# Loading and transposing x by row tile at the start of a cached-attention kernel

## The chip, the core and the metric

The kernel runs on one core of a Trainium2 chip. The metric is the device time of one execution in microseconds. A profile is one further execution with the hardware profiler on; its times are in microseconds from the start of its span.

## What is computed

The reference is attention over the last W keys of a cache, with a projection in front and one behind. All tensors are bf16.

```python
B, Sq, D = 8, 32, 1024;  Hq, Hkv, Sk, Dh = 32, 4, 8192, 128
W = min(4096, max(256, Sk // 4))                     # 2048
q = (x @ wq).reshape(B, Sq, Hq, Dh).transpose(0, 2, 1, 3)
k = repeat(k_cache[:, :, Sk - W:, :], Hq // Hkv, axis=1)   # v alike
p = softmax(einsum("bhqd,bhkd->bhqk", q, k) * Dh ** -0.5)
o = einsum("bhqk,bhkd->bhqd", p, v)
return o.transpose(0, 2, 1, 3).reshape(B, Sq, Hq * Dh) @ wo
```

x has 256 rows (8 batches of 32) of 1024 values, so it is two row tiles of 128 rows.

## The kernel before

The work is cut into 32 units, one for each pair of KV group g and batch b, with all batches of a group in a row. A unit has 16 key tiles of 128, taken in four chunks of four. A chunk is four score matmuls (L467), one exponential on ScalarE (L469), and eight matmuls that apply the result to the values (L478). The value matmuls of a chunk are queued two chunks behind its scores. Beside them the loop in `run` puts in other TensorE work at fixed places: transposes of K for the next unit (`k_pieces`, L236), the q projection of later groups (`q_pieces`, L275) and the output projection (`o_pieces`, L295).

The order of every engine's instructions is the order in which the program writes them (`manual_schedule`). Nearly all loads are issued on SP's queue, one behind the other; `start` writes down the first ones: x, the eight c-blocks of `wq` for group 0 in seven pieces (L164: four of one block, one of two, two of one), K and V of the first units (L188, L193, L204). One half of x goes over ScalarE's queue instead. An issue on SP can wait until an earlier transfer has landed or until a buffer is free, and everything behind it on SP then waits too. K of units 0 to 4 is loaded as it is and transposed on TensorE; K of unit 4 is read by the pieces at L236 during unit 3.

`start` is the part around the change. Ahead of any data, TensorE runs eight matmuls on constants (`warm_up`, L346) into a PSUM tile `warm_ps`. x is in `x_sb`, 128 rows of each row tile on the partitions. `x_turn` (L350) transposes it in blocks of 128 × 128: a c-block takes the columns c, c + 8, c + 16 and so on. The first call does c = 0 to 3 of both row tiles into one PSUM tile, the second c = 4 to 7 into another; in each, VectorE copies the first two c-blocks to `xT` and ScalarE the other two (L357). Then come the q matmuls of group 0 (L375): for c = 0 to 7, eight heads each, with `wq` as the stationary and `xT` of both row tiles as the moving operand, and into four PSUM tiles of two heads (L361). For c = 6 and 7 (`Q_CUT`) only row tile 0 is done at first, and the rest of it in `q_rest`. Ahead of c = 6 the first half of unit 0's K is transposed (`k_turn`, L368).

PSUM comes from three pools of two buffers, `ps_m` (tag `m`), `ps_o` and `ps_s` (tag `s_ps`). A buffer is handed out again when all readers of its last tile are done. `warm_ps` has one of `ps_s`; the first `xT_ps` has one of `ps_m`, the second the other of `ps_s`.

Of the kernel before, what the change touches and what calls it, by code (L numbers as in the profile page):

```python
# [11 lines left out]
BF16 = mybir.dt.bfloat16  # L12
# [4 lines left out]
RL_LIMIT = 1.0e22  # L17
RL_MIN = 1.0e-10
Q_CUT = 6
N_WARM = (8, 0, 0)  # L20
VA_ROW = 160
V_HALVES = 30

# [81 lines left out]
class Fast:  # L105
# [206 lines left out]
    def start(self):  # L312
        nc, P = self.nc, self.P
        warm = self.ps_s.tile([P, 512], FP32, name="warm_ps", tag="s_ps")
        one = nc.const_aps.tensor
        x_sb = self.vp.tile([P, self.NT, self.D], BF16, name="x_sb", tag="v")
        xf = self.x.rearrange("b s d -> (b s) d")
        H = self.DC // 2

        nc.sync.dma_start(out=x_sb[:, 0, :], in_=xf[0:P, :])  # L320
        nc.scalar.dma_start(out=x_sb[:, 1, :], in_=xf[P:2 * P, :])
        wq0 = self.load_wq(0, 0, (1, 1, 1, 1)) + self.load_wq(0, 1, (2, 1, 1))
        for p in wq0[:5]:
            p()
        self.load_k(0, 0)
        wq0[5]()
        wq0[6]()
        self.load_k(0, 1)
        self.load_v(0, nc.sync)
        self.load_k(1)  # L330
        self.load_v(1, nc.sync)
        self.weights = []
        for g in range(self.Hkv):
            if g + 1 < self.Hkv:
                self.weights += self.load_wq(g + 1, 0) + self.load_wq(g + 1, 1)
            if g:
                self.weights += self.load_wo(2 * g - 2) + self.load_wo(2 * g - 1)
        self.weights += self.load_wo(2 * self.Hkv - 2) + self.load_wo(2 * self.Hkv - 1)
        for ui in range(2, 4):
            self.load_unit(ui)  # L340
        for v in self.va:
            nc.gpsimd.memset(v[:, :, self.Dh:self.VW], 1.0)
        nc.gpsimd.memset(self.ones_c[:, :], 1.0)
        def warm_up(n):
            for i in range(n):
                nc.tensor.matmul(warm[:, :], lhsT=one(1.0, [P, P], BF16), rhs=one(1.0, [P, 512], BF16), start=True, stop=True)  # L346
        warm_up(N_WARM[0])


        def x_turn(half, pl, tag):  # L350
            ps = pl.tile([P, H, self.NT, P], BF16, name="xT_ps", tag=tag)
            for c in range(H):
                for t in range(self.NT):
                    nc.tensor.transpose(ps[:, c, t, :], x_sb[:, t, half * H + c:self.D:self.DC], self.ident[:, :])
            for i, copy in ((0, nc.vector.tensor_copy), (1, nc.scalar.copy)):
                c0 = half * H + i * H // 2
                copy(out=self.xT[:, c0:c0 + H // 2, :], in_=ps[:, i * H // 2:(i + 1) * H // 2, :, :].rearrange("p c t s -> p c (t s)"))  # L357

        x_turn(0, self.ps_m, "m")
        x_turn(1, self.ps_s, "s_ps")  # L360
        qs = [pl.tile([P, 2, self.NQ], FP32, name="q0_ps", tag=tag)  # L361
              for pl, tag in ((self.ps_o, "o_ps"), (self.ps_o, "o_ps"), (self.ps_m, "m"), (self.ps_m, "m"))]
        KT = self.KT
        tp = None

        def k_turn(half):
            for j in range(half * KT // 2, (half + 1) * KT // 2):
                nc.tensor.transpose(tp[:, j, :], self.k_raw[0][:, j, :], self.ident[:, :])  # L368

        def k_copy(half):  # L370
            sl = slice(half * KT // 2, (half + 1) * KT // 2)
            nc.vector.tensor_copy(out=self.kT[0][:, sl, :], in_=tp[:, sl, :])

        def q_mm(c, h, n0, n1):
            nc.tensor.matmul(qs[h // 2][:, h % 2, n0:n1], lhsT=self.wq_t[0, c // H][:, c % H, h * P:(h + 1) * P],  # L375
                             rhs=self.xT[:, c, n0:n1], start=(c == 0 and h % 2 == 0), stop=(c == self.DC - 1),
                             skip_group_check=True)

        for c in range(self.DC):
            for h in range(self.rep):  # L380
                q_mm(c, h, 0, P if c >= Q_CUT else self.NQ)
            if c == 0:
                warm_up(N_WARM[2])
                warm_sb = self.c1.tile([P, 8], BF16, name="warm_sb")
                nc.vector.tensor_copy(out=warm_sb[:, :], in_=warm[:, 0:8])
            if c == self.DC - 3:
                tp = self.ps_s.tile([P, KT, P], BF16, name="kf_ps", tag="s_ps")
                k_turn(0)
                k_copy(0)
        k_turn(1)  # L390

        def q_copy(eng, k, b0, b1):
            src = qs[k][:, :, :].rearrange("p h (b s) -> p b h s", b=self.B)[:, b0:b1, :, :]
            dst = self.q_view(0)[:, b0:b1, k * 2:(k + 1) * 2, :]
            (nc.vector.tensor_copy if eng == "v" else nc.scalar.copy)(out=dst, in_=src)
        for k, eng in ((0, "a"), (1, "v"), (2, "a"), (3, "v")):
            q_copy(eng, k, 0, 1)
        k_copy(1)
        self.va_copy(0)

        def q_rest(k):
            for h in (2 * k, 2 * k + 1):
                for c in range(Q_CUT, self.DC):
                    q_mm(c, h, P, self.NQ)
            q_copy("v", k, 1, self.B)
        self.q_rest = [lambda k=k: q_rest(k) for k in (0, 2, 3, 1)]
# [249 lines left out]
```

## Time and profile before

| | us |
|---|---|
| median of 9 runs | 185.82 |
| lowest and highest | 185.38, 187.02 |
| the profiled execution, its own time | 186.01 |
| its span | 184.23 |
| TensorE busy in the span | 179.6 |
| first warm-up matmul starts | 0.78 |
| x issued on ScalarE's queue and on SP's | 0.74, 0.75 |
| time from these issues to landing | 3.4, 3.2 |
| first transpose of x | 4.06 |
| first q matmul of group 0 | 5.39 |
| first score matmul of unit 0 | 13.21 |

In the rows of a profile PE is TensorE's matmuls and PEld its weight loads, which overlap with them; DVE is VectorE, ACT ScalarE, POOL GpSimd. SPq and ACTq are the queues' issues of transfers. A row of the timeline has the start, the length, the engine, the source line, the operation with the tile written and the tiles read, the shapes and the number of instructions taken together; square brackets hold the idle time before it and what ended it. A row of the chain has the start, the length, and the engine or transfer. Matmuls are pipelined and their ends are modelled, so the distance between starts tells more than the lengths.

### The profile page before, as it was taken

The page shows a single profiled execution, that of the slowest core. Times are in us where ns is not written, and L with a number is a line of the kernel's source. Part 1 is how long each engine was busy: PE and PEld are TensorE (multiplying, and loading weights), DVE is VectorE, ACT ScalarE, POOL GpSimd, SP SyncE. Part 2 cuts the span into 40 slices and gives each one's busy share as a digit, 9 for nine tenths or more (in the row PEclk, how much of TensorE's full clock was granted, in tenths as well). Part 3 has the DMA queues.
Part 4 walks back from the last instruction along what each step waited for, and adds up shares of the span by engine and source line. Part 5 has one row for each costly group of instructions (what it writes and reads, how often), then busy time and mean ns, then how long its engine had stood idle before and what let it go on. Part 6 is the DMA issues. An engine that isn't in the chain of part 4 may idle for free.

```text
span 184.2 us, 5057 instructions
## 1 busy us (share of the span) xinstructions
PE 179.6 (97%) x2057; PEld 153.6 (83%) x2057; DVE 115.1 (62%) x266; ACT 131.6 (71%) x133; POOL 94.6 (51%) x150
## 2 busy tenths in 40 slices
PE   8999999999999999999999999999999999999993
PEld 3789998999999999987878999988787888888843
DVE  0138899995585685586467558646755865365363
ACT  2208998776889787878777677787877888888800
POOL 2000009749939959929954980796299279600000
PEclk9999999999999999999999999999999999999999
DMA  6999999999999999999999999999999999820013
GB/s 195 338 410 406 398 402 368 193 193 363 263 360 257 366 278 315 403 257 243 377 380 240 367 389 254 297 382 290 258 368 332 231 367 304 210 51 0 0 35 89
DMA packets 52954, 51.73 MB, mean 281 GB/s; under 512 B 39744, under 2 KB 40256, under 8 KB 52928
## 3 DMA queue, kind: packets, MB, share of 16 engines
q1 hardware_dynamic: 52352, 50.90, 97.4%
q10 hardware_dynamic: 576, 0.49, 0.8%
q8 instruction: 16, 0.26, 0.6%
q14 instruction: 10, 0.08, 0.2%
HBM read 41.42 MB, written 0.52 MB: 228 GB/s over the span
## 4 chain that ended last, share of the span: by engine, by line
PE 83%; DMA 14%; SPq 1%; issue 0%; DVE 0%
PE o_ps L478 29%; PE s_ps L467 27%; PE op_ps L295 15%; PE q_ps L275 11%; DMA k_raw<-in_k_cache_dram 6%; DMA v_sb<-in_v_cache_dram 5%; DMA wq_sb<-in_wq_dram 3%; SPq L164 1%; PE tp L236 1%; SPq L320 0%; DVE o_t L305 0%; PE cnt_ps L532 0%
## 5 line engine op out<-in xcount | busy, mean ns | idle before, releaser
L469 ACT ACTIVATE pT<-s_ps 128x1024 bf16<-128x1024 f32 x128 | 128.8, 1025 | 33.0 <-PE s_ps L467 32.1
L261 POOL TENSOR_SCALAR kTv<-kb 32x512 bf16<-32x512 bf16 x140 | 93.6, 669 | 64.8 <-PE s_ps L467 38.3
L478 PE MATMUL o_ps<-va,pT 128*128 128x129 bf16 x1024 | 78.8, 220 | 0.0
L478 PEld LDWEIGHTS <-pT 128*128 128x128 bf16 x1024 | 68.5, 98 | 3.1
L467 PE MATMUL s_ps<-QT,kT 128*128 128x256 bf16 x368 | 55.2, 273 | 0.0
L467 PEld LDWEIGHTS <-kT 128*128 128x128 bf16 x368 | 34.8, 98 | 10.4
L295 PE MATMUL op_ps<-wo_sb,OT 128*128 128x512 bf16 (+2 forms) x144 | 36.2, 355 | 0.0
L275 PE MATMUL q_ps<-xT,wq_sb 128*128 128x256 bf16 x192 | 28.1, 273 | 0.0
L409 DVE COPY va<-v_sb 128x2048 bf16<-128x2048 bf16 x32 | 25.3, 789 | 0.1
L251 DVE STREAM_TRANSPOSE kb<-k_raw 128x512 bf16<-128x512 bf16 x36 | 23.8, 685 | 0.0
L415 DVE RECIPROCAL RL_all<-o_ps 128x2 f32<-128x2 f32 x32 | 5.3, 165 | 27.8 <-PE o_ps L478 27.7
L467 PE MATMUL s_ps<-QT,kTv 128*128 128x256 bf16 x144 | 21.6, 272 | 0.0
L420 DVE TENSOR_SCALAR o_sb<-o_ps,RL_all 128x128 bf16<-128x128 f32 x64 | 19.5, 347 | 1.1
L467 PEld LDWEIGHTS <-kTv 128*128 128x128 bf16 x144 | 13.9, 98 | 5.1
L278 DVE CAST QT<-q_ps 128x256 bf16<-128x256 f32 x24 | 9.8, 406 | 13.4 <-PE q_ps L275 13.4
L275 PEld LDWEIGHTS <-wq_sb 128*128 128x128 bf16 x192 | 17.0, 98 | 1.2
L422 DVE STREAM_TRANSPOSE OT<-o_sb 128x256 bf16<-128x256 bf16 x32 | 14.3, 446 | 1.1
L295 PEld LDWEIGHTS <-OT 128*128 128x128 bf16 x144 | 11.4, 98 | 2.3 <-DVE OT L422 0.2
L302 DVE TENSOR_TENSOR oacc<-op_ps,oacc 128x512 f32<-128x512 f32 x8 | 5.5, 683 | 7.4 <-PE op_ps L295 7.4
L375 PE MATMUL q_ps<-xT,wq_sb 128*128 128x256 bf16 (+1 forms) x80 | 7.8, 251 | 0.6 <-DMA wq_sb<-in_wq_dram 0.6
L375 PEld LDWEIGHTS <-wq_sb 128*128 128x128 bf16 x80 | 6.6, 98 | 1.5 <-DMA wq_sb<-in_wq_dram 0.9
L236 PE MATMUL tp<-ident,k_raw 128*128 128x128 bf16 x64 | 5.9, 219 | 0.4 <-DMA k_raw<-in_k_cache_dram 0.4
(30 smaller groups left out, 36.7 us busy)
## 6 DMA issues: line engine op xcount, KB each, us to landing
v_sb<-in_v_cache_dram SPq DMA_DIRECT2D x30, 512.0 KB, 6.8
wo_sb<-in_wo_dram SPq DMA_DIRECT2D x16, 512.0 KB, 6.2
wq_sb<-in_wq_dram SPq DMA_DIRECT2D x13, 512.0 KB, 7.4
k_raw<-in_k_cache_dram SPq DMA_DIRECT2D x13, 512.0 KB, 5.8
wq_sb<-in_wq_dram SPq DMA_DIRECT2D x6, 256.0 KB, 4.7
v_sb<-in_v_cache_dram SPq DMA_DIRECT2D x4, 256.0 KB, 4.2
kT<-in_k_cache_dram SPq DMA_TRANSPOSE x36, 6.4
k_raw<-in_k_cache_dram SPq DMA_DIRECT2D x2, 256.0 KB, 6.9
```

The lines of the kernel that those rows point to most:

```text
L251: nc.vector.transpose(out=st["kb"][:, sl, :], in_=self.k_raw[ui][:, sl, :])
L261: nc.gpsimd.tensor_scalar(out=out, in0=in_, scalar1=1.0, scalar2=1.0, op0=ALU.mult, op1=ALU.mult)
L275: nc.tensor.matmul(st["ps"][:, 0:self.NQ], lhsT=self.wq_t[g, i][:, c % (DC // 2), hl * P:(hl + 1) * P], rhs=self.xT[:, c, :], start=(c == ...
L278: nc.vector.tensor_copy(out=self.q_view(g)[:, :, hl, :], in_=st["ps"][:, 0:self.NQ].rearrange("p (b s) -> p b s", b=self.B))
L295: nc.tensor.matmul(ps[:, 0:w], lhsT=self.OT[:, gq, c, t * P:(t + 1) * P], rhs=self.wo_t[gq][:, c, n0:n0 + w], start=(k == 0), stop=(k == 7))
L375: nc.tensor.matmul(qs[h // 2][:, h % 2, n0:n1], lhsT=self.wq_t[0, c // H][:, c % H, h * P:(h + 1) * P], rhs=self.xT[:, c, n0:n1], start=(c ...
L409: self.nc.vector.tensor_copy(out=self.va[ui % 3][:, :, 0:self.Dh], in_=self.v_sb[ui][:, :, :])
L420: nc.vector.tensor_scalar(out=o_sb[:, qt, :, :], in0=o_ps[:, qt, 0:Dh].rearrange("p (i c) -> p c i", c=4), scalar1=rl[:, ui * QT_N + qt:ui ...
L422: nc.vector.transpose(out=self.OT[:, g * QT_N:(g + 1) * QT_N, :, b * self.Sq:(b + 1) * self.Sq], in_=o_sb[:, :, :, :])
L467: nc.tensor.matmul(s_ps[:, jj, :], lhsT=self.kT[ui][:, c * CJ + jj, :], rhs=q_u, start=True, stop=True)
L469: nc.scalar.activation(out=pT[:, :, :], in_=s_ps[:, :, :], func=ACT.Exp, bias=0.0, scale=self.scale)
L478: nc.tensor.matmul(o_ps[:, qt, 0:self.VW], lhsT=pT[:, jj, qt * P:(qt + 1) * P], rhs=va[:, j, 0:self.VW], start=(j == 0 and qt == 0), stop= ...
```

## The change

x is loaded in four transfers of 64 rows: for row tile 0 one on SP's queue (rows 0 to 63) and one on ScalarE's (rows 64 to 127), then the same for row tile 1. The transposes go by row tile. Row tile 0 has all eight c-blocks in one PSUM tile of `ps_s`, copied half by VectorE and half by ScalarE; row tile 1 has c = 0 to 3 in one tile of `ps_m`, copied by VectorE, and c = 4 to 7 in another tile of `ps_m`, copied by ScalarE. The warm-up has seven matmuls, and the copy that reads its result comes straight behind it instead of behind the q matmuls of c = 0.

```diff
-N_WARM = (8, 0, 0)
+N_WARM = 7
...
-        nc.sync.dma_start(out=x_sb[:, 0, :], in_=xf[0:P, :])
-        nc.scalar.dma_start(out=x_sb[:, 1, :], in_=xf[P:2 * P, :])
+        for t in range(self.NT):
+            for eng, p0 in ((nc.sync, 0), (nc.scalar, P // 2)):
+                eng.dma_start(out=x_sb[p0:p0 + P // 2, t, :], in_=xf[t * P + p0:t * P + p0 + P // 2, :])
...
-        warm_up(N_WARM[0])
-
-
-        def x_turn(half, pl, tag):
-            ps = pl.tile([P, H, self.NT, P], BF16, name="xT_ps", tag=tag)
-            for c in range(H):
-                for t in range(self.NT):
-                    nc.tensor.transpose(ps[:, c, t, :], x_sb[:, t, half * H + c:self.D:self.DC], self.ident[:, :])
-            for i, copy in ((0, nc.vector.tensor_copy), (1, nc.scalar.copy)):
-                c0 = half * H + i * H // 2
-                copy(out=self.xT[:, c0:c0 + H // 2, :], in_=ps[:, i * H // 2:(i + 1) * H // 2, :, :].rearrange("p c t s -> p c (t s)"))
-
-        x_turn(0, self.ps_m, "m")
-        x_turn(1, self.ps_s, "s_ps")
+        warm_up(N_WARM)
+        warm_sb = self.c1.tile([P, 8], BF16, name="warm_sb")
+        nc.vector.tensor_copy(out=warm_sb[:, :], in_=warm[:, 0:8])
+
+
+        def x_turn(t, c0, c1, pl, tag, copies):
+            ps = pl.tile([P, self.DC, P], BF16, name="xT_ps", tag=tag)
+            for c in range(c0, c1):
+                nc.tensor.transpose(ps[:, c - c0, :], x_sb[:, t, c:self.D:self.DC], self.ident[:, :])
+            n = (c1 - c0) // len(copies)
+            for i, copy in enumerate(copies):
+                copy(out=self.xT[:, c0 + i * n:c0 + (i + 1) * n, t * P:(t + 1) * P], in_=ps[:, i * n:(i + 1) * n, :])
+
+        x_turn(0, 0, self.DC, self.ps_s, "s_ps", (nc.vector.tensor_copy, nc.scalar.copy))
+        x_turn(1, 0, H, self.ps_m, "m", (nc.vector.tensor_copy,))
+        x_turn(1, H, self.DC, self.ps_m, "m", (nc.scalar.copy,))
...
-            if c == 0:
-                warm_up(N_WARM[2])
-                warm_sb = self.c1.tile([P, 8], BF16, name="warm_sb")
-                nc.vector.tensor_copy(out=warm_sb[:, :], in_=warm[:, 0:8])
```

## The prediction

> **What bounds the kernel now.** I read the page first, then the chain of work in order of time, then the timeline of the first 30 us. The page:
>
> ```profile
> PE 179.6 (97%) x2057; PEld 153.6 (83%) x2057; DVE 115.1 (62%) x266; ACT 131.6 (71%) x133; POOL 94.6 (51%) x150
> PE 83%; DMA 14%; SPq 1%; issue 0%; DVE 0%
> ```
>
> TensorE is busy for 179.6 of 184.2 us, yet 14% of the chain, about 26 us, is DMA. The chain in order of time says where:
>
> ```profile
> 2.60 4.78 DMA wq_sb<-in_wq_dram
> 7.39 9.67 DMA v_sb<-in_v_cache_dram
> 17.07 10.95 DMA k_raw<-in_k_cache_dram
> 28.07 0.40 PE tp L236 x4
> ```
>
> Three transfers hand over to each other, each issued when the one before lands, and from 28.07 on everything is TensorE. The table of stretches shows that the transfers are limited by their rate (the columns after the stretch are its length, the engines, the TensorE clock, the DMA share, GB/s):
>
> ```profile
> 2.50:6.50 4.00, 3.98 (x32) 2.58 (x31) 0.92 (x3) 1.08 (x2) 0.00 (x0) 1.00 1.03 376
> 23.00:28.00 5.00, 4.67 (x68) 4.31 (x65) 4.90 (x11) 4.64 (x5) 0.61 (x2) 1.00 1.03 401
> 28.00:60.00 32.00, 31.93 (x400) 29.94 (x401) 24.25 (x57) 25.99 (x27) 23.68 (x35) 1.00 1.17 285
> ```
>
> From 2.5 to 28 us all 16 DMA engines are busy (share about 1); after 28 TensorE is (31.93 of 32). So the end is set by the landing at 28.02 of unit 4's `k_raw`, plus 156 us of TensorE work without a gap. Where does TensorE stand before that? The timeline:
>
> ```profile
> 4.03 1.20 PEld L354 LDWEIGHTS <-x_sb 128*128 128x128 bf16 x16 [0.58 <-DMA x_sb<-in_x_dram]
> 4.06 1.31 PE L354 MATMUL xT_ps<-ident,x_sb 128*128 128x128 bf16 x16
> 4.91 0.92 DVE L357 COPY xT<-xT_ps 128x512 bf16<-128x512 bf16 x2 [4.91 <-PE xT_ps L354]
> 5.37 1.08 ACT L357 COPY xT<-xT_ps 128x512 bf16<-128x512 bf16 x2 [2.91 <-DVE xT L357]
> 5.39 3.65 PE L375 MATMUL q_ps<-xT,wq_sb 128*128 128x256 bf16 x32
> 9.62 1.92 PE L375 MATMUL q_ps<-xT,wq_sb 128*128 128x256 bf16 x16 [0.58 <-DMA wq_sb<-in_wq_dram]
> 27.05 0.62 PE L478 MATMUL o_ps<-va,pT 128*128 128x129 bf16 x8
> 28.07 0.40 PE L236 MATMUL tp<-ident,k_raw 128*128 128x128 bf16 x4 [0.40 <-DMA k_raw<-in_k_cache_dram]
> ```
>
> TensorE stands still for DMA twice after x: before 9.62 for the third `wq` piece of two rows (c = 4, 5), and before 28.07. The records show 0.58 and 0.40; their ends are modelled. By spacing: 32 matmuls in 3.65 us with a last one of 0.27 start 0.109 apart, so issue ends at 8.88 and **0.74** is idle; eight `o_ps` matmuls at 0.056 end at 27.50, so **0.57** is idle.
>
> This gives the two rules of the sum. TensorE earlier at the front is worth nothing: it waits longer at 9.62 and 28.07. TensorE later is free up to 0.74 + 0.57 = 1.31 us. But a shift of the DMA stream reaches the end one to one.
>
> **The change part by part.**
>
> *SP's queue: one more x issue* (64 rows of row tile 1). No 64-row issue is in the trace. Bounds: 0 and the 128-row x issue, 0.39, with its 0.06 gap; I take 0.45, since other 128-row issues of other sizes take 0.33 to 0.47. Behind it stand the `wq` issues at 1.20 to 3.51, then `k_raw`, `wq`, `v_sb`. Are engines left without work? x's first packets move at 1.8 to 2.5 and the stream is full from 2.5; the first `wq` is now issued at 1.65 instead of 1.20, about 2 us ahead of the end of x's packets (3.6). No. And SP's lead is soon gone anyway, because its issues wait for landings:
>
> ```profile
> 6.10 0.33 SPq L204 DMA_DIRECT2D v_sb<-in_v_cache_dram  x1
> 6.74 0.43 SPq L193 DMA_DIRECT2D k_raw<-in_k_cache_dram  x1
> 7.39 0.34 SPq L204 DMA_DIRECT2D v_sb<-in_v_cache_dram  x1
> 9.59 0.33 SPq L193 DMA_DIRECT2D k_raw<-in_k_cache_dram  x1
> 10.26 0.33 SPq L204 DMA_DIRECT2D v_sb<-in_v_cache_dram  x1
> ```
>
> Each of these comes at the landing of the transfer eight places before it (7.39: the `wq` issued at 2.60, as in the chain). SP is idle from 5.69 to 6.10, so 0.41 of the 0.45 is swallowed there. With two more x transfers in that rotation, the two-row `wq` and the first `k_raw` half (3.07 and 3.55 now) come to wait for the first x pieces, which I expect at 3.4 to 3.65 against their own shifted times of 3.52 and 4.0: at most 0.1. Later issues wait for the same landings as before. The `v_sb` at 6.10 slips by 0.1 at most, with about 2 MB queued ahead of it. Path: 0. Without that cover it would be 0.45.
>
> *ACT's queue: one more x issue*, 0.40, ahead of ACT's table load (1.18 to 2.46 now, 2.9 then). ACT's first copy comes after 4.5. Path: 0.
>
> *The stream itself: two more transfers, same bytes, same 2 KB packets.* Nearest rows: SP's issues above date the landings: 256 KB each 0.67 (9.59 to 10.26), while 512 KB takes 1.28 (17.07 to 18.36 by SP's rows). Two halves cost 1.34, so one more transfer costs 0.06; two, 0.12. A smaller first issue could start the stream up to half of its 0.39 earlier, -0.2. Bounds -0.2 and +0.12; I take **+0.05**, nearer to the row that shows a cost.
>
> Here a rule speaks against the change. The Trainium skill, SBUF — State Buffer, "Can I just issue two DMAs to hit both halves?", says that 64 partitions reach half of the ports, and that two concurrent transfers to the two halves gained only 6% over one. Then x's 512 KB, 1.3 us at 400 GB/s (rows above), would take some 2.6 us and push the whole stream by 1.3: end +1.3. By the trace, two queues already share the engines evenly (x lands on SP after 3.2 and on ACT after 3.4 us), which is a sign that halves on two queues run side by side. No row here has 64 partitions, so I use the row's value and keep +1.3 as a rival.
>
> *Warm-up: 8 to 7 matmuls.* They start 0.427 apart (3.44 us for eight); the eighth starts at 3.72. TensorE is then free at 3.72 instead of about 4.05: -0.33 before the transposes, all ahead of the 0.74 slack.
>
> *Transposes by row tile.* Still 16, now 0.062 apart (1.31 less the last 0.23, over 15, is 0.072; the first two are slow). Half of x's packets are through by about 3.1, and landings trail the last packet by 0.5 (x: packets to 3.6, landed by 4.1), so row tile 0 lands at about 3.6, row tile 1 at 4.1 as now. Tile 0: 3.75 to 4.3, results at 4.5. DVE copies four blocks 4.55 to 4.98 (0.425 as now), ACT the other four after it, 0.587, since today ACT also starts only when DVE leaves the same PSUM tile: 5.0 to 5.6. Tile 1: transposes 4.3 to 4.8; DVE 5.0 to 5.43, ACT 5.6 to 6.2. The first `q_ps` matmul needs DVE's second copy: 5.45 instead of 5.39. Heads 6 and 7 of c = 0 write a PSUM buffer that ACT's second copy frees: at 5.45 + 6 × 0.109 = 6.1 they wait 0.1. Front: 0.06 + 0.1 = **0.16 later**, from bounds of -0.3 (tile 1 lands earlier) and +0.4 (both tiles land together at 4.17). All within the 0.74. The warm-up's reading copy (DVE, 0.15) now comes at 3.95, while DVE is idle until 4.55: 0; uncovered it would be 0.15.
>
> *Sum* for the profiled execution: span 184.23 + 0 (front, hidden) + 0.05 (stream) = 184.28; what lies around the span stays 186.01 - 184.23 = 1.78; so 186.06. The median of the nine runs is 0.19 under that execution: **185.87, told as 185.9**.
>
> **The rivals.**
>
> *A. As worked out: nothing to speak of.* Includes the case that row tile 0 does not land ahead at all; the front is then 0.4 later, still hidden. Own range 185.5 to 186.3.
>
> *B. The clock stays low: slower.* Place: the transposes and first `q_ps` matmuls. Warm-up matmuls of 512 columns take 0.427 each, `q_ps` ones of 256 take 0.109, so TensorE doubles its pace at about 4.0, during the eighth warm-up, although the page's granted clock reads 1.00 throughout. That matmul goes, and transposes stand in its place. TensorE: Matmul & The Clock Gate, "Part 4: PE-mode transpose", of the Trainium skill says that transposes don't count as busy in the same way; Part 1 there has windows of 3.4 us. Then the step would come at 7.4 or 10.8. Cold transposes: 16 × 0.045 = 0.7, less what is cold now, 0.5; cold `q_ps` matmuls 0.213. TensorE is late by 0.16 + 0.5 + half of the time from 5.9 to the step. It decides once this passes 1.31, that is at a step after 7.2: +0.1 for 7.4, +1.8 for 10.8, giving 187.6. For it: the loss of the eighth matmul, and 0.5 us in which TensorE now waits for copies. Against it: seven matmuls keep it busy from 0.78 to 3.72 and transposes follow at once. The trace can't tell, as transposes before the step number two at most.
>
> *C. Halves serialise: slower.* +1.3 on the stream: 187.1. It decides when x's last piece lands later than about 4.7, which the 0.56 us below would show.
>
> *D. The stream starts earlier: faster.* If the ramp from 1.8 to 2.5 vanished, -0.6: 185.2. For it: smaller first issues. Against: first packets of about 0.6 us each, which smaller transfers don't shorten.
>
> **How the numbers follow.** Chances: A 0.62, B 0.15, C 0.15, D 0.08. A measurement of this kernel can't tell changes under 0.3%, 0.56 us, from none. B stays inside it where the step comes at 7.4 (0.03); A leaves it on either side at 0.02 to 0.03; D gives 0.08 to faster. So faster 0.10, same 0.60, slower 0.30. The range has A whole, C and the milder half of B: 185.3 to 187.1; it leaves out about half of D and the worst of B and C.
>
> **What would show it.** Right: `k_raw` of unit 4 lands within 0.15 of 28.02, TensorE waits for it, and has no idle time after it; the first `q_ps` matmul within 0.3 of 5.39; a wait for `wq` still ahead of c = 4. B: `q_ps` matmuls 0.21 apart after 5.4. C: x pieces landing after 4.7 and every landing behind them late by the same amount. D: packets at full rate before 2.4. It would be wrong if SP's issues left engines idle before 6 us, or if a later wait depends on the start's PSUM order.

## The result, and the profile after

The changed kernel is slower: 187.68 us median (18 executions, 186.48 to 189.61) beside 185.85 us for the kernel before (55 executions), ratio 1.0079, 95% interval 1.0059 to 1.0098. By the ratio that is about 1.5 us; the two medians themselves lie 1.83 apart. Either way it is outside the range of 185.3 to 187.1, and not the "no change" that was forecast.

One more profile belongs ahead of everything else, because it changes how the first one is read. The kernel before was profiled a second time (its run is told below). Its chain of work in order of time:

```profile
0.78 3.57 PE warm_ps L346 x8
4.35 1.71 PE xT_ps L354 x16
6.06 5.29 PE q_ps L375 x48
11.36 0.45 PE kf_ps L368 x8
```

There is no transfer in it. TensorE runs from the first warm-up matmul on, through all 48 q matmuls up to c = 5, without a wait for `wq`. This execution's span is 183.7 us; the median is 183.6 in the 11 executions beside it and 183.7 in 55 others. The profile that the prediction was made from has 184.2, and only 17 of the 120 executions beside the runs below have as much. Its waits of 0.74 and 0.57 us, counted there as slack, were mostly that one execution's own. A third profile of the same program (in the probe below, which adds loads only behind the last output) has waits of 0.19 for `wq` and of 0.36 and 0.20 for `k_raw`.

The chain of the changed kernel, in order of time, goes over transfers, as in the first profile of before, but leaves them at 20.00 instead of 28.07:

```profile
4.06 6.63 DMA wq_sb<-in_wq_dram
10.70 9.25 DMA k_raw<-in_k_cache_dram
20.00 0.40 PE tp L236 x4
```

Its timeline, with the issues (SPq, ACTq) and TensorE's rows:

```profile
0.75 1.22 SPq L322 DMA_DIRECT2D x_sb<-in_x_dram  x2
0.75 1.48 ACTq L322 DMA_DIRECT2D x_sb<-in_x_dram  x2
2.01 2.48 SPq L164 DMA_DIRECT2D wq_sb<-in_wq_dram  x5
4.01 1.07 PE L356 MATMUL xT_ps<-ident,x_sb 128*128 128x128 bf16 x8
5.65 0.71 PE L356 MATMUL xT_ps<-ident,x_sb 128*128 128x128 bf16 x8 [0.57 <-DMA x_sb<-in_x_dram]
6.62 3.77 PE L378 MATMUL q_ps<-xT,wq_sb 128*128 128x256 bf16 x32 [0.27 <-DVE xT L359]
10.73 1.92 PE L378 MATMUL q_ps<-xT,wq_sb 128*128 128x256 bf16 x16 [0.33 <-DMA wq_sb<-in_wq_dram]
29.08 0.40 PE L236 MATMUL tp<-ident,k_raw 128*128 128x128 bf16 x4
29.08 0.23 PEld L236 LDWEIGHTS <-k_raw 128*128 128x128 bf16 x4 [0.18 <-DMA k_raw<-in_k_cache_dram]
```

The rows to compare, from the second profile of before:

```profile
4.15 1.91 PE L354 MATMUL xT_ps<-ident,x_sb 128*128 128x128 bf16 x16
5.86 5.50 PE L375 MATMUL q_ps<-xT,wq_sb 128*128 128x256 bf16 x48
27.69 0.40 PE L236 MATMUL tp<-ident,k_raw 128*128 128x128 bf16 x4
27.69 0.23 PEld L236 LDWEIGHTS <-k_raw 128*128 128x128 bf16 x4 [0.18 <-DMA k_raw<-in_k_cache_dram]
```

Two issues of 64 rows take 1.22 us on SP and 1.48 us on ACT, where one of 128 rows took 0.39 and 0.40. SP reaches the first `wq` at 2.01 instead of 1.20. The last piece of x lands at 5.6 instead of 4.2 (ACT's second issue at 1.36 with 4.2 to landing, against 0.74 with 3.4). The first q matmul starts at 6.62 instead of 5.86, the ones for c = 4 at 10.73 instead of about 9.4 (5.86 + 32 × 0.109), unit 4's K is transposed from 29.08 instead of 27.69. In both profiles the last wait of TensorE's weight loads for a transfer is this one, 0.18 us, for unit 4's `k_raw`, which lands at 29.04 instead of 27.64. From there on TensorE runs in parallel in the two traces, 1.39 us apart up to its last matmuls (177.87 beside 176.49). So TensorE's loss is complete by 29 us, and it is of the size that the ratio says (0.0079 × 185.85 = 1.47). The two spans differ by 1.8; the other 0.4 lies behind TensorE's last matmuls and wasn't followed.

The table of stretches shows the stream. After the stretch come its length, the busy times of PE, PEld, DVE, ACT and POOL, the TensorE clock, the DMA share and GB/s. The changed kernel:

```profile
2.50:5.00 2.50, 2.42 (x12) 1.06 (x10) 0.17 (x1) 1.05 (x1) 0.00 (x0) 1.00 0.86 267
5.00:11.00 6.00, 4.83 (x44) 3.79 (x44) 0.85 (x2) 1.17 (x2) 0.00 (x0) 1.00 0.98 327
11.00:28.00 17.00, 16.88 (x240) 15.98 (x237) 12.97 (x28) 11.88 (x14) 0.00 (x0) 1.00 1.03 405
```

The kernel before, second profile:

```profile
2.50:5.00 2.50, 2.50 (x13) 1.29 (x12) 0.00 (x0) 0.00 (x0) 0.00 (x0) 1.00 0.97 314
5.00:11.00 6.00, 6.00 (x57) 5.44 (x56) 0.92 (x3) 1.17 (x2) 0.00 (x0) 1.00 1.02 368
11.00:28.00 17.00, 16.97 (x245) 15.97 (x243) 14.32 (x30) 13.18 (x15) 0.61 (x1) 1.00 1.03 405
```

Up to 11 us the changed kernel moves 47 GB/s less over 2.5 us and 41 GB/s less over 6 us: 0.12 + 0.25 = 0.36 MB, 0.9 us at 405 GB/s. From 11 us on both run at 405 and the lag stays. (The rest of the 1.39 was not parted. Some of it lies ahead of 2.5 us: 31 GB/s beside 56 from 0 to 2.5.)

### The profile page after: what moved, and what is told of

Same layout as the page of the kernel before. It is cut to its first block, busy times and chain, and to the rows that moved or that the text cites. A ratio compares the mean times of both kernels' runs of the same rounds, so it can differ in the third digit from the quotient of the medians.

```text
span 185.5 us, 5059 instructions
## 1 busy us (share of the span) xinstructions
PE 180.3 (97%) x2056; PEld 153.6 (83%) x2056; DVE 115.7 (62%) x266; ACT 131.6 (71%) x133; POOL 94.6 (51%) x150
## 4 chain that ended last, share of the span: by engine, by line
PE 88%; DMA 9%; SPq 2%; issue 0%; DVE 0%
PE o_ps L477 31%; PE s_ps L466 29%; PE op_ps L295 15%; PE q_ps L275 11%; DMA k_raw<-in_k_cache_dram 5%; DMA wq_sb<-in_wq_dram 4%; PE tp L236 2%; SPq L164 1%; SPq L322 1%; DVE o_t L305 0%; PE cnt_ps L531 0%
## 5 line engine op out<-in xcount | busy, mean ns | idle before, releaser
L408 DVE COPY va<-v_sb 128x2048 bf16<-128x2048 bf16 x32 | 26.1, 816 | 0.1
L295 PEld LDWEIGHTS <-OT 128*128 128x128 bf16 x144 | 11.4, 98 | 2.3 <-DVE OT L421 0.2
```

The source lines that it names most:

```text
L295: nc.tensor.matmul(ps[:, 0:w], lhsT=self.OT[:, gq, c, t * P:(t + 1) * P], rhs=self.wo_t[gq][:, c, n0:n0 + w], start=(k == 0), stop=(k == 7))
L408: self.nc.vector.tensor_copy(out=self.va[ui % 3][:, :, 0:self.Dh], in_=self.v_sb[ui][:, :, :])
```

## The experiments

Three theories were set against each other. **S**: the 64-row loads slow the start of the stream and the landing of x. **P**: the two halves of the partitions don't move side by side (rival C). **T**: the transposes by row tile, the copies and the lost warm-up matmul (rival B). In the measured lines, "span" is the median of the executions that the ratio compares; beside it stands that of the kernel before on the same chip. It scatters less than the whole time, of which some 1.9 us lie outside the span.

### One part alone, one part undone

The kernel before with the four loads alone:

```diff
-        nc.sync.dma_start(out=x_sb[:, 0, :], in_=xf[0:P, :])
-        nc.scalar.dma_start(out=x_sb[:, 1, :], in_=xf[P:2 * P, :])
+        for t in range(self.NT):
+            for eng, p0 in ((nc.sync, 0), (nc.scalar, P // 2)):
+                eng.dma_start(out=x_sb[p0:p0 + P // 2, t, :], in_=xf[t * P + p0:t * P + p0 + P // 2, :])
```

> The kernel before with only the four 64-row loads of x. Theory S (starved stream): a 64-row issue takes some 0.58 us instead of at most 0.39, SP reaches the first wq at 2.0 instead of 1.2, DMA engines idle between 3.0 and 4.5, and every landing behind is about 1.0 late: unit 4's k_raw lands near 29.0, ratio 1.005 to 1.009. Rival P (ports: the two halves of the partitions don't move side by side): the same time, but the engines stay busy and packets take longer than 0.084. Rival T (transposes by row tile, cold clock, copies): this part costs nothing, k_raw at 28.0, ratio 0.999 to 1.002.

Measured: ratio 1.0135 (1.0099 to 1.0172), span 186.25 beside 183.7, more than S expected. The loads cost more alone than in the change. Unit 4's `k_raw` did land at 28.8, as S said, but TensorE came to it only at 30.3:

```profile
4.13 0.22 PE L355 MATMUL xT_ps<-ident,x_sb 128*128 128x128 bf16 x1
6.14 1.12 PE L355 MATMUL xT_ps<-ident,x_sb 128*128 128x128 bf16 x15 [1.79 <-DMA x_sb<-in_x_dram]
7.30 5.87 PE L376 MATMUL q_ps<-xT,wq_sb 128*128 128x256 bf16 x37
7.30:9.00 1.70, 1.70 (x9) 1.25 (x9) 0.50 (x2) 1.06 (x2) 0.00 (x0) 0.56 1.03 375
9.00:11.00 2.00, 2.00 (x12) 1.44 (x10) 0.00 (x0) 0.00 (x0) 0.00 (x0) 0.52 1.00 313
```

Here the second transpose waits for x till 6.14, and the first 37 q matmuls (the row ends at 13 us) take 5.87 us, so many of them run at the low pace (at 0.109 apart they would take 4.2). The granted clock shows it: 0.56 and 0.52 up to 11 us (the last but two columns of the stretches). Two of the six executions have such a lower clock over the whole span (0.991) and spans of 186.7 and 187.2; the other four, at 1.0, have 186.0 to 186.3. So the low clock adds to the loss but doesn't make it.

The changed kernel with the loads undone (the diff above, reversed, in the changed kernel):

> The changed kernel with the two whole loads of before. S and P: the stream is as before, k_raw of unit 4 at 28.0, ratio 0.998 to 1.002, although TensorE's first q matmul may be up to 0.7 later. T: the loss stays, ratio 1.005 to 1.009.

Measured: 1.0008 (0.9988 to 1.0029), span 183.8 beside 183.7. The first q matmul starts at 6.07:

```profile
6.07 5.61 PE L377 MATMUL q_ps<-xT,wq_sb 128*128 128x256 bf16 x48
```

So the loads carry the whole loss; the row-tile order, the copies and seven warm-up matmuls cost nothing by themselves (T falls). With the late x they are even of use: the change as a whole is 0.7 us better (185.5) than the loads alone (186.25).

### Shape, number or place of the transfers

Four loads, none with 64 rows (in the kernel before, in place of the two lines removed above, as in the next ones):

```diff
+        for t in range(self.NT):
+            for eng, d0 in ((nc.sync, 0), (nc.scalar, self.D // 2)):
+                eng.dma_start(out=x_sb[:, t, d0:d0 + self.D // 2], in_=xf[t * P:(t + 1) * P, d0:d0 + self.D // 2])
```

> The kernel before with four loads of x that each span 128 partitions and half of the columns (1 KB rows): as many transfers as in the change, none with 64 rows. S in the form that the price hangs on the 64-row shape: issues of about 0.39, first wq at 1.65, k_raw of unit 4 at 28.0 to 28.3, ratio 1.000 to 1.002. S in the form that the price hangs on the number of issues in flight on two queues: issues near 0.58 again, k_raw near 29, ratio above 1.004. P: no loss.

Measured: 1.0039 (1.0016 to 1.0061), span 184.25 beside 183.7. The issues take 0.39 to 0.45 us, x lands between 3.5 and 4.3. The first `wq` piece lands at 6.1 instead of 5.2. The loss is above the 1.002 expected for the form with the 64-row price, and below the 1.004 of the other: the number of transfers explains a part, no more.

Two loads of 64 rows, each with both row tiles:

```diff
+        for eng, p0 in ((nc.sync, 0), (nc.scalar, P // 2)):
+            eng.dma_start(out=x_sb[p0:p0 + P // 2, :, :],
+                          in_=xf.rearrange("(t p) d -> p t d", p=P)[p0:p0 + P // 2, :, :])
```

> The kernel before with two loads of x of 64 rows, each with both row tiles (SP rows 0 to 63, ACT rows 64 to 127). The 64-row shape without more transfers. S with a price per 64-row issue: first wq at 1.4 to 1.6, so a loss of 0 to 0.4: k_raw of unit 4 at 28.0 to 28.4, ratio 1.000 to 1.002. P: as bad as the change, k_raw near 29, ratio 1.005 to 1.009.

Measured: 1.0096 (1.0062 to 1.0131), span 185.15 beside 183.8, by four executions that scatter from 184.2 to 186.1. As many transfers and bytes as before, each on half of the partitions: the issues take 0.76 and 0.71 us, and SP's half of x lands at 5.6. The 64-row shape costs without any additional transfer. The profiled execution is one of the better ones (184.4), and its `k_raw` of unit 4 lands at 28.3, so this expectation was right about the landing and wrong about the time.

Four 64-row loads in other pairs, so that both queues write the same half of the partitions at a time:

```diff
+        for p0 in (0, P // 2):
+            for t, eng in ((0, nc.sync), (1, nc.scalar)):
+                eng.dma_start(out=x_sb[p0:p0 + P // 2, t, :], in_=xf[t * P + p0:t * P + p0 + P // 2, :])
```

> The kernel before with four 64-row loads, but SP has both halves of row tile 0 and ACT both of row tile 1, so that both queues write the same half of the partitions at the same time. S: as in the load alone, since issues and queues are the same in number and shape: k_raw of unit 4 near 29, ratio 1.005 to 1.009. P: clearly worse than the load alone, as only half of the ports work at a time: x lands after 5.5 and k_raw over 29.5, ratio above 1.010.

Measured: 1.0122 (1.0099 to 1.0145), span 186.45 beside 183.8; x's two last pieces land at 5.5 and 5.9, unit 4's `k_raw` at 28.6. The ratio and x are where P expected them, but the load alone is there too (1.0135, 6.1): this is no worse than the load alone.

Four 64-row loads on every second partition:

```diff
+        for t in range(self.NT):
+            for eng, p0 in ((nc.sync, 0), (nc.scalar, 1)):
+                eng.dma_start(out=x_sb[p0:P:2, t, :], in_=xf[t * P + p0:(t + 1) * P:2, :])
```

> The kernel before with four 64-row loads of x, each of every second partition (SP the even ones, ACT the odd ones), so that each transfer reaches across all 128 partitions. If the loss comes from a transfer being confined to one half of the partitions, it goes: x lands by 4.5, ratio 1.000 to 1.004. If it comes from 64 rows to a transfer, whatever their place, it stays: issues of 0.58 on SP, last piece of x after 5.5, ratio 1.010 to 1.016 like the load alone.

Measured: 1.015 (1.0112 to 1.0188), span 186.4 beside 183.6. In the profile the last piece of x lands at 5.2 and the two-row `wq` piece at 11.4, later than in the changed kernel. Reaching across all partitions doesn't help. Together with the pairs this speaks against P: where the 64 rows lie makes no difference, that there are 64 does.

The price by itself. Behind the last output of the kernel before, x is loaded again into a spare tile, in eight shapes, on SP alone and then beside ACT:

```diff
         self.last[3](mm=False)
         for p in self.last[6:]:
             p()
+        pa = self.wp.tile([P, 4, self.D], BF16, name="pa", tag="w")
+        for k in range(8):
+            probe(nc.sync, pa, k)
...
```

> The kernel before with a row of further loads of x into a spare tile behind its last output, first on SP alone, then on SP and ACT side by side: 128 rows; 128 rows of half the columns; 64 rows (0 to 63, 64 to 127, every second); 64 rows of both row tiles; 32 rows; 96 rows. Its time is longer by these loads and isn't compared; only the issues' lengths count. If the price hangs on the rows of a transfer, 64-row issues on SP alone take 0.5 to 0.6 as against 0.4 for 128 rows, wherever the rows lie. If it comes from two queues issuing 64-row transfers at once, they take under 0.4 alone and 0.58 side by side.

Rows of the timeline and of the transfers' landing for SP's queue, each issued after the landing of the one before it, the last with a transfer of ACT's beside it. The first column is the start, the second the length of the issue; the second kind of row ends with the time from the issue to the landing. In order: 128 rows of half the columns (184.50), every second row of 128 (189.86), 64 rows of both row tiles (192.37), 96 rows (197.64), 128 rows in whole (202.75):

```profile
184.50 0.33 SPq L531 DMA_DIRECT2D pa<-in_x_dram  x1
pa<-in_x_dram SPq DMA_DIRECT2D x1, 128.0 KB, 2.0
189.86 0.49 SPq L531 DMA_DIRECT2D pa<-in_x_dram  x1
pa<-in_x_dram SPq DMA_DIRECT2D x1, 128.0 KB, 2.5
192.37 0.67 SPq L531 DMA_DIRECT2D pa<-in_x_dram  x1
pa<-in_x_dram SPq DMA_DIRECT2D x1, 256.0 KB, 3.5
197.64 0.32 SPq L531 DMA_DIRECT2D pa<-in_x_dram  x1
pa<-in_x_dram SPq DMA_DIRECT2D x1, 192.0 KB, 2.3
202.75 0.35 SPq L531 DMA_DIRECT2D pa<-in_x_dram  x1
pa<-in_x_dram SPq DMA_DIRECT2D x1, 256.0 KB, 2.6
```

64 rows are slow to issue (0.49 to 0.67) and slow to land: 2.5 us for 128 KB against 2.0 in the full-width shape, 3.5 us for 256 KB against 2.6. Issues of 32 rows (0.33 to 0.35), 96 rows (0.32 to 0.33) and 128 rows (0.33 to 0.46, the longest two beside other traffic) are quicker. The packets of this trace show where most of the late landing lies: the first 2 KB packet of 64 rows starts 1.3 us behind the start of the issue (1.5 for both row tiles), the first packet of 32, 96 or 128 rows 0.9 to 1.0. The packets themselves then take little longer in all: 0.87 us from first to last for every second row, 0.75 for the same bytes over 128 rows. SP and ACT side by side gave the same lengths (64 rows of one row tile: 0.48 to 0.61), so it isn't the second queue.

### What the stream waits for

Only the first `wq` issue later, by one whole x issue on SP (the second line of x on `nc.sync`):

```diff
-        nc.scalar.dma_start(out=x_sb[:, 1, :], in_=xf[P:2 * P, :])
+        nc.sync.dma_start(out=x_sb[:, 1, :], in_=xf[P:2 * P, :])
```

> The kernel before with both whole loads of x on SP's queue: only the first wq issue is put back, by one 128-row issue, to 1.65. S says the engines have x's 512 KB to work on meanwhile, so little is lost: k_raw of unit 4 at 28.0 to 28.4, ratio 1.000 to 1.002. If the stream loses in proportion to the delay of the first wq (1.0 for 0.8), it is 0.55: k_raw at 28.6, ratio 1.003. P and T: no loss.

Measured: 1.0029 (1.001 to 1.0048), span 184.0 beside 183.7: 0.3 us by the span, 0.5 by the ratio, for an issue that the sum had hidden. That is the second of the two sizes expected.

All four 64-row loads on ACT's queue, so that SP issues `wq` from 0.75 on (in the kernel before, in place of the two lines):

```diff
+        for t in range(self.NT):
+            for eng, p0 in ((nc.scalar, 0), (nc.scalar, P // 2)):
+                eng.dma_start(out=x_sb[p0:p0 + P // 2, t, :], in_=xf[t * P + p0:t * P + p0 + P // 2, :])
```

> The kernel before with the four 64-row loads of x all on ACT's queue, so that SP issues wq from 0.75 on. If the stream starves because SP reaches wq late, it is full here from 2.5: over 900 KB moved by 5.0 us, the two-row wq piece lands by 9.3, and only x is late (after 5.5), ratio 1.008 to 1.016 through TensorE's late front. If the 64-row transfers hold up the engines themselves, under 750 KB have moved by 5.0 and the two-row wq piece lands after 10.

Measured: 1.0315 (1.0282 to 1.0349), span 190.2 beside 183.9, twice what was expected. x lands as late as 9.7, which goes far to explain the time; two of the four executions have a lower granted clock as well (0.982) and are 1.0 us longer than the others. The stream:

```profile
2.50:5.00 2.50, 1.85 (x5) 0.39 (x3) 0.00 (x0) 1.28 (x1) 0.00 (x0) 1.00 0.97 258
5.00:11.00 6.00, 1.41 (x12) 1.33 (x13) 0.18 (x1) 0.00 (x0) 0.00 (x0) 0.73 1.05 300
```

By 3.3 us 1.5 MB had been issued, by 5.0 only some 0.8 MB had moved (158 GB/s from 0 to 5.0), between the two marks of the expectation, and the two-row `wq` piece landed at 10.8. The engines are recorded as busy (0.97), at 258 GB/s. So a late SP isn't the only cause: work was there, and it moved slowly while 64-row transfers were among it. This run doesn't part the two wholly, since from 2.7 to 5.0 SP itself waited for a piece of x to land before it could issue more.

### Is a late TensorE hidden?

Both whole loads of x behind the first two `wq` pieces, in the kernel before:

```diff
+        wq0 = self.load_wq(0, 0, (1, 1, 1, 1)) + self.load_wq(0, 1, (2, 1, 1))
+        for p in wq0[:2]:
+            p()
         nc.sync.dma_start(out=x_sb[:, 0, :], in_=xf[0:P, :])
-        nc.scalar.dma_start(out=x_sb[:, 1, :], in_=xf[P:2 * P, :])
-        wq0 = self.load_wq(0, 0, (1, 1, 1, 1)) + self.load_wq(0, 1, (2, 1, 1))
-        for p in wq0[:5]:
+        nc.sync.dma_start(out=x_sb[:, 1, :], in_=xf[P:2 * P, :])
+        for p in wq0[2:5]:
             p()
```

> The kernel before with both whole loads of x on SP behind the first two pieces of wq. The stream keeps its start and its bytes, only x lands later, near 5.4, as in the changed kernel. By the sum in the prediction a TensorE that starts 1.2 later is hidden by the waits of 0.74 and 0.57: ratio 1.000 to 1.002. If the second wait (for unit 4's k_raw) is not there in most executions, as the run with the wq pieces moved suggests, 0.4 to 0.8 of it shows: ratio 1.002 to 1.005.

Measured: 1.0185 (1.0153 to 1.0216), span 186.7 beside 183.6. Its profile:

```profile
6.57 1.82 PE L356 MATMUL xT_ps<-ident,x_sb 128*128 128x128 bf16 x15 [1.11 <-DMA x_sb<-in_x_dram]
8.18 6.31 PE L377 MATMUL q_ps<-xT,wq_sb 128*128 128x256 bf16 x48
```

x lands at 6.5, 2.3 later than before, the first q matmul starts at 8.18 instead of 5.86, and the first eight take 1.7 us where 0.87 is the high pace. So the q matmuls end 3.1 later (14.49 instead of 11.36). The stream was undisturbed (unit 4's `k_raw` at 27.7). TensorE comes to that transfer 2.8 later (30.46 instead of 27.69): 0.4 of the late start is hidden, the two short waits for `k_raw` in the second profile of before, and nothing like 1.31.

The kernel before, profiled again:

> The kernel before, unchanged, for a second profile. If the wait of 0.57 for unit 4's k_raw near 28 us was a matter of that one execution, it is absent or under 0.2 here and the span is near 183.7, the median span of 55 executions; if it belongs to the kernel, it is 0.4 to 0.6 again and the span near 184.2.

Measured: span 183.7. TensorE waits for `k_raw` twice, 0.4 us by the table of waits, the longer one 0.2; ahead of unit 4 it starts at 27.69 when eight matmuls from 27.07 end at 27.52, so 0.17. (The weight loads show 0.20 and 0.18.) The wait of 0.57 belonged to the first profile.

The first two `wq` pieces of group 1 behind unit 4's `k_raw`, in the kernel before and in the changed one:

```diff
-W_AT = (3, 3, 4, 4, 8, 8, 9, 9, 11, 12, 13, 13, 14, 15, 16, 16, 18, 19, 19, 20, 22, 22, 23, 24, 25, 26, 28, 28)
+W_AT = (4, 4, 4, 4, 8, 8, 9, 9, 11, 12, 13, 13, 14, 15, 16, 16, 18, 19, 19, 20, 22, 22, 23, 24, 25, 26, 28, 28)
```

> The kernel before with the first two wq pieces of group 1 issued behind unit 4's and unit 8's k_raw instead of ahead of unit 4's. Tests that the landing of unit 4's k_raw sets the end: it comes some 2.6 earlier, at about 25.4, TensorE has no wait there, and the end is 0.4 to 0.57 earlier: ratio 0.997 to 0.998. If the end hangs on something else, 1.000.

> The changed kernel with the same move of two wq pieces. The wait for unit 4's k_raw goes, but TensorE itself is late from the front (third wq piece and unit 2's k_raw land 1.1 to 1.6 later), so only 0.1 to 0.3 is won on the changed kernel: ratio to the kernel before 1.004 to 1.008. If the landing of unit 4's k_raw alone carried the loss, it would fall to 1.000.

Measured: in the kernel before 1.001 (0.9994 to 1.0027), span 183.8 beside 183.8; in the changed kernel 1.0098 (1.0073 to 1.0123), span 185.65. The `k_raw` did come early (24.7 and 25.2) and nothing was won. In the kernel before, the landing of unit 4's `k_raw` holds up the end by no more than the short wait of 0.18, if at all; the expected gain of 0.4 to 0.57 didn't come. In the changed kernel TensorE, late from the front, comes to that transfer at 29.43 without a wait (29.08 in the profile of the change): there both are late, and mending the stream alone at this place gains nothing.

### TensorE's pace, and a combination

Ten warm-up matmuls in the changed kernel, two of them between the row tiles (the copy that reads their result moves behind these two):

```diff
-        warm_up(N_WARM)
+        warm_up(8)
...
         x_turn(0, 0, self.DC, self.ps_s, "s_ps", (nc.vector.tensor_copy, nc.scalar.copy))
+        warm_up(2)
         x_turn(1, 0, H, self.ps_m, "m", (nc.vector.tensor_copy,))
```

> The changed kernel with eight warm-up matmuls ahead of row tile 0 and two more between the transposes of row tile 0 and row tile 1, where TensorE otherwise waits for x. If part of the loss is TensorE's low pace after these waits (16 transposes at 0.107 instead of 0.062, q matmuls at 0.21 instead of 0.109 in some executions), the median span falls from 185.5 by 0.4 to 0.8 and the ratio to the kernel before is 1.003 to 1.006. If the late landing of x and of the transfers behind it is all, the ratio stays at 1.007 to 1.010.

Measured: 1.0091 (1.0064 to 1.0118), span 185.45 beside 183.6. In its profile the q matmuls run at the high pace from the first one on, and still nothing is won, as x landed at 6.6 there (5.6 in the profile of the change; why it was later wasn't found). In the profile of the change, too, the q matmuls run at the high pace, 0.109 apart, from the first one on. The pace is not the main part of the loss of the change.

Row-tile order with full-width loads, eight warm-up matmuls and the moved `wq` pieces (in the changed kernel in place of its loop over the loads, `W_AT` as above):

```diff
+        h = self.D // 2
+        nc.sync.dma_start(out=x_sb[:, 0, 0:h], in_=xf[0:P, 0:h])
+        nc.scalar.dma_start(out=x_sb[:, 0, h:], in_=xf[0:P, h:])
+        nc.scalar.dma_start(out=x_sb[:, 1, :], in_=xf[P:2 * P, :])
```

> Transposes by row tile as in the change, with eight warm-up matmuls, the two wq pieces of group 1 moved behind unit 4's k_raw, and x in three transfers of 128 partitions: row tile 0 in two halves of its columns, one on each queue, row tile 1 whole on ACT, so that SP turns to wq after one issue as before. If the start is bound by x and then by TensorE, row tile 0 lands near 3.6, row tile 1 near 4.3, the first q matmul comes at 5.4 to 5.7 instead of 5.86, and the span is 0 to 0.3 under the kernel before's 183.7: ratio 0.998 to 1.000. If the wq landings bind it, no gain: 1.000 to 1.002.

Measured: 1.0011 (0.9988 to 1.0034), span 184.1 beside 183.9. Row tile 0 landed at 3.5, but row tile 1 at 5.0 and the first q matmul started at 6.24. No version here beats the kernel before.

## Why the prediction was wrong

**The step that failed: the stream's "+0.05".** By the prediction's own rule a shift of the DMA stream reaches the end one to one. It put two more transfers at 0.05, from rows of 128 partitions (0.06 for one more transfer). Unit 4's `k_raw` landed at 29.04 instead of the 28.02 of that profile and the 27.64 of the second one, 1.0 to 1.4 late. The 64-row loads carry this: undone they leave a ratio of 1.0008, alone they give 1.0135, and four loads of full width give 1.0039. Two answers led to the small number.

The issue of a 64-row piece was bounded by "0 and the 128-row x issue, 0.39". It took 0.57 to 0.59 on SP, and on ACT 0.58 and 0.87. Half of the rows was taken to cost at most the whole; there was no row for the shape, and the rows of 96, 32 and 128 measured since show that the price doesn't rise with the rows.

"Are engines left without work? No." The DMA share from 2.5 to 5 us fell to 0.86 and the rate to 267 GB/s; that SP's issues leave engines idle before 6 us is what the prediction itself named as a sign of being wrong. Even one whole issue more on SP, with x's bytes to work on, cost 0.3 us of the span, so "Path: 0" for SP's queue was wrong by that much.

**The step that failed beside it: "TensorE later is free up to 0.74 + 0.57 = 1.31 us."** Both numbers were read rightly, but from one execution. In the second profile of the same kernel the first wait is absent and the second is 0.18, with another of 0.20 ahead of it; with x late by 2.3 us the end was late by 3.1, and 0.4 was hidden. In the two later profiles of this kernel TensorE and the stream arrive at 28 us nearly together, so that a loss on either shows in all but a few tenths, and in the changed kernel both are late. A hint was there: the profiled execution's waits made it longer, and nothing in the text asked whether other executions had them.

**The landings.** Row tile 0 was expected at 3.6 and landed by 3.96; row tile 1 was expected at 4.1 and landed at 5.6. With that the first q matmul came at 6.62 instead of 5.45.

**What held.** The transposes, copies and the shorter warm-up: expected front 0.16 later and no loss; measured with the loads undone, first q matmul at 6.07 against 5.86, ratio 1.0008.

**Rival C** had the sign, nearly the time (187.1) and the sign by which to tell it: x's last piece after 4.7, with every landing behind it late. Its reason didn't hold. It rested on the Trainium skill's page SBUF — State Buffer, "Can I just issue two DMAs to hit both halves?", by which only a transfer over all 128 partitions reaches all 16 ports. Here 64 rows on every second partition were as slow, and two queues on the same half were no slower than on different halves. The page's advice, not to split a load into halves, agrees with the times; where it puts the cause, these runs don't follow. The trace row preferred to it (x's two 128-row transfers landing together) said nothing about 64 rows.

**Rival B** happens, but is not what made this change slow: its sign, q matmuls 0.21 apart after 5.4, is absent from the changed kernel's profile (0.109). In the changed kernel's profile row tile 0's eight transposes take 1.07 us for 0.71 of row tile 1's, so the pace rose between them; and in the second profile of before all 16 transposes take 1.91 for 1.31 in the first. The pace of the first 2 us differs from execution to execution in both kernels. It adds to the loss in profiles where TensorE waited long for x: with the loads alone, and with x behind `wq`.

**Open.** Why 64 rows in particular are slow wasn't found. The longer issue is not all of it, as the landing is late by more (0.5 us for 128 KB, 0.9 for 256 KB), over half of it ahead of the first packet. How much of the late stream comes from SP's late `wq` and how much from slow transfers was not parted. Nor was what each of the two late arrivals in the changed kernel, x at 5.6 and the first `wq` piece at 5.9, would cost without the other. The nearest runs have `wq` late and x in time (first `wq` piece at 6.1, span +0.55; at 5.7, +0.3) and x late and `wq` in time (x at 6.5, +3.1).

## What to carry to other kernels

A wait of half a microsecond in one profile is slack only if other executions have it too: compare that execution's span with the median of many, or take a second profile, before work is hidden behind it. Bound an operation that the trace doesn't show by a row of the same shape, not by a larger one, and where none is there, let the upper end be well above the nearest row. At a kernel's start, when everything waits for the first bytes, load in the shape that is quickest to issue and land, and split it only after the split pieces have been timed by themselves.

## What was not expected of the hardware

A transfer of 64 rows of 2 KB took longer to issue (0.48 to 0.61 us) than one of 32, 96 or 128 rows (0.32 to 0.35 with nothing beside it) and landed later than 128 rows with the same bytes (2.5 against 2.0 us), on either queue and wherever the rows lay. At the start the granted clock in the stretches reads 1.00 while transposes of the same shape run at 0.107 or at 0.062 us apart (the second and the first profile of before), and with x behind `wq` it reads 1.00 while q matmuls run at 0.21; with the loads alone it reads 0.56 and 0.52 at that pace. So the start's pace has to be read from the distance between starts.
